# Chunked attention in 256-token units with one head per half of the array's rows, ahead of a soft mixture of experts

## The chip, the cores and the metric

The kernel runs on one core of a Trainium2 chip. The core has five engines with their own instruction queues: TensorE (in profiles PE for matmuls and PEld for weight loads), VectorE (DVE), ScalarE (ACT), GpSimd (POOL) and SyncE (SP), which here only issues DMA transfers. Sixteen DMA engines move data between HBM and SBUF. Matmuls write PSUM, eight banks of 2 KB on each of 128 partitions. The metric is the device time of one execution in microseconds; less is better.

## What is computed

All data is fp32: 4 batches, 8 heads, 768 tokens, head dimension 64. The first half is attention in chunks of 32 queries. A chunk sees 8 memory keys of its head and the tokens from 16 before the chunk to 8 after it, 64 keys in all away from the sequence's ends.

```python
for c in range(nc):                                  # 24 chunks of 32
    l_start = max(0, c_start - left_ctx)             # 16 before
    r_end = min(S, c_end + right_ctx)                # 8 after
    k_full = np.concatenate([mem_k, k[:, :, l_start:r_end]], axis=2)
    v_full = np.concatenate([mem_v, v[:, :, l_start:r_end]], axis=2)
    scores = scale * np.matmul(q_c, k_full.transpose(0, 1, 3, 2))
    a = softmax(scores)
    out[:, :, c_start:c_end] = np.matmul(a, v_full)
```

The second half takes the 3072 tokens x (512 wide) through 8 experts with 4 slots each:

```python
logits = x @ phi                                     # 3072 x 32
d = softmax over tokens (axis 0); slot_input = d.T @ x
h = np.maximum(slot_input[e] @ w1[e], 0.0)           # 512 -> 1024, per expert
slot_out[e] = h @ w2[e]                              # 1024 -> 512
return softmax over slots (axis 1) of logits @ slot_out
```

The two weight arrays have 16.8 MB each, the output 6.3 MB.

## The kernel before

The attention loop (line 362) runs over 24 units of 128 tokens, four chunks each, with all eight heads. Keys lie in `k_slab` with the two heads of a pair interleaved over the 128 partitions (`par`), and each head's columns hold zeros on the other head's partitions. So one matmul in `scores` (line 218) contracts over 128 rows and gives the scores of two heads for one chunk: 32 queries by 2 x 64 keys, into a strip of 32 output partitions. There are 16 such matmuls per unit, four head pairs by four chunks. `values` (line 271) is built in the same way with `v_slab`. Per unit follow: four transposes of the probabilities (`transpose_p`, copied out of PSUM by ScalarE), the row maximum, the subtraction, the sum and its reciprocal on VectorE, the exponent on ScalarE, the normalization into `x_slab` on VectorE and four transposes of x. Every fourth unit there are logits and, one and two units later, the dispatch of four units' tokens with a running maximum per slot.

Neighbouring chunks share value rows. `share_v` (line 129) copies 64 partitions of a unit, on VectorE for even units and on ScalarE for odd ones.

PE, DVE, ACT and SP keep the order in which the program is written (`InOrder`); GpSimd's few operations and all waits come from the framework, which puts semaphores on data. `scores(i + 2)` runs two units ahead of `values(i)`.

All loads are issued by SP in one order. Inputs arrive as queries for two units (`load_q`), keys for three (`load_k`, two transfers on every other partition each) and values for two (`load_v`, four transfers on every other partition). At the end of each iteration `load_w` issues weight pieces of 512 KB: 13 slabs are free from the start, filled at 0.9 piece per unit, and from unit 18 on the input slabs that are no longer needed are taken as well, 38 pieces in all. The other 26 wait until the experts have read the pieces of w1 whose slabs they take.

At the start GpSimd, VectorE and ScalarE clear the padded slabs (lines 188 to 198). After the loop come the last group's dispatch (lines 400 to 453), the experts' first layer (`expert_in`), the combine weights, and per half of the output columns the second layer (`expert_out`) and the combine, which ends in the output transfers. `keep_warm` puts matmuls on zeros between them.

```python
load_w(usable[i] if i >= NU - 6 else min(NW, W0 + int(WRATE * max(0, i + 1 - WSTART))))
```

Of the kernel before, what the change touches and what calls it, by code (L numbers as in the profile page):

```python
# [10 lines left out]
F32 = mybir.dt.float32  # L11
# [10 lines left out]
CPU = P // CHUNK  # L22
UPB = S // P
NU = B * UPB
HALF_U = 3
NHALF = NU // HALF_U
SPAN_STEP = CPU // 2 * (NMEM + 2 * CHUNK)
SPAN_EXTRA = LEFT + RIGHT
STREAM = (S // CHUNK // 2) * (NMEM + 2 * CHUNK) + SPAN_EXTRA
HALF_W = HALF_U * SPAN_STEP + SPAN_EXTRA  # L30
# [12 lines left out]
PIECE = 1024  # L43
NW = 13
NV = 3
W0 = 1
SHARE_MOD = 2
SHARE_DVE = 1
WARM0 = 3
FILL = (4, 2, 6, 2, 2)  # L50
WARM1 = 1
# [19 lines left out]
def window_start(c):  # L71
    return (c // 2) * (NMEM + 2 * CHUNK) + (c % 2) * CHUNK


@with_exitstack
def tile_attn_softmoe(
    ctx: ExitStack,
    tc: tile.TileContext,
    qT: bass.AP,
    kT: bass.AP,  # L80
    vw: bass.AP,
# [7 lines left out]
    pe, dve, act, sp = (InOrder(tc, e) for e in (nc.tensor, nc.vector, nc.scalar, nc.sync))  # L89
    cp = ctx.enter_context(tc.tile_pool(name="cp", bufs=1))  # L90
    wk = ctx.enter_context(tc.tile_pool(name="wk", bufs=2))
    ps = ctx.enter_context(tc.tile_pool(name="ps", bufs=2, space=bass.MemoryType.PSUM))

    k_slab = [cp.tile([P, 2, NPAIR, HALF_W], F32, tag=f"k{i}", name=f"k{i}") for i in range(2)]
    v_slab = [cp.tile([P, 2, 2, 2, 2, NPAIR, D], F32, tag=f"v{i}", name=f"v{i}") for i in range(NV)]
    q_slab = [cp.tile([P, 2, NPAIR, P], F32, tag=f"q{i}", name=f"q{i}") for i in range(3)]
# [4 lines left out]
    hT = cp.tile([P, E, NFC, NSLOT], F32, tag="hT", name="hT")  # L101
# [4 lines left out]
    phi_sb = cp.tile([P, NKC, NSLOT], F32, tag="phi", name="phi_sb")  # L106

    def load_q(p):
        sp.dma_start(q_slab[p % 3], qT[p])

    def load_k(hb, lo=0, hi=HALF_W):
        b, half = divmod(hb, 2)
        off = half * HALF_U * SPAN_STEP - LEFT
        if half and lo == 0:
            nc.gpsimd.tensor_copy(
                out=k_slab[1][:, :, :, 0:SPAN_EXTRA], in_=k_slab[0][:, :, :, HALF_W - SPAN_EXTRA:HALF_W]
            )
        lo = max(lo, SPAN_EXTRA if half else LEFT)
        hi = min(hi, HALF_W - RIGHT if half else HALF_W)
        for par in range(2):  # L120
            sp.dma_start(k_slab[half][par:P:2, par, :, lo:hi], kT[b, :, par, :, off + lo:off + hi])
# [495 lines left out]
```

## Time and profile before

| | us |
|---|---|
| median of 3 runs | 190.63 |
| lowest and highest | 189.44, 194.12 |
| profiled execution, first to last instruction | 193.7 |
| PE busy in it | 154.5 |
| DVE busy | 122.1 |
| ACT busy | 77.9 |
| POOL busy | 19.4 |

The profile lists one execution by its span; the time of that execution as a whole is not listed apart from the three runs. TensorE's mean granted clock was 0.942 of full speed. 63.11 MB went through the DMA queues at a mean of 326 GB/s.

The page cuts the span into 40 slices and gives each engine's busy share in tenths. A group line names the engine, the operation, what it writes and reads (out<-in), the shapes and the count, then busy time, mean ns of one, and the idle time ahead of it with what ended that. "issue" as a releaser means that the engine waited for nothing that the profile shows. Matmul ends are modelled, so times between the starts of neighbouring groups are the safer measure. Nearly all operations carry line 66, that of the helper which records them; they are told apart by tile names: s scores, p probabilities, pt their transposes, a values, x and xT tokens, l logits, D dispatch, h and so the experts' two layers, o the combine.

### The profile page before, as it was taken

The page shows a single profiled execution, that of the slowest core. Times are in us where ns is not written, and L with a number is a line of the kernel's source. Part 1 is how long each engine was busy: PE and PEld are TensorE (multiplying, and loading weights), DVE is VectorE, ACT ScalarE, POOL GpSimd, SP SyncE. Part 2 cuts the span into 40 slices and gives each one's busy share as a digit, 9 for nine tenths or more (in the row PEclk, how much of TensorE's full clock was granted, in tenths as well). Part 3 has the DMA queues.
Part 4 walks back from the last instruction along what each step waited for, and adds up shares of the span by engine and source line. Part 5 has one row for each costly group of instructions (what it writes and reads, how often), then busy time and mean ns, then how long its engine had stood idle before and what let it go on. Part 6 is the DMA issues. An engine that isn't in the chain of part 4 may idle for free.

```text
span 193.7 us, 6125 instructions
## 1 busy us (share of the span) xinstructions
PE 154.5 (80%) x2637; PEld 108.0 (56%) x2637; DVE 122.1 (63%) x249; ACT 77.9 (40%) x137; POOL 19.4 (10%) x22
## 2 busy tenths in 40 slices
PE   6733997859996969989579996999899769599540
PEld 3313775737684737757457684767466535365330
DVE  4699999829999649989936997243742220370550
ACT  8003457415756434763445577220322220160240
POOL 8991000000000000000000000000311100000000
PEclk9995899978999999999978999999999978999995
DMA  5999969998899999889978999999999999999296
GB/s 154 305 276 285 287 188 292 343 320 298 278 279 329 344 337 326 254 271 354 261 231 240 335 394 418 409 405 409 412 405 409 409 407 408 409 415 401 85 376 273
DMA packets 21194, 63.11 MB, mean 326 GB/s; under 512 B 2992, under 2 KB 7600, under 8 KB 21168
## 3 DMA queue, kind: packets, MB, share of 16 engines
q1 hardware_dynamic: 21168, 62.73, 92.8%
q8 instruction: 21, 0.34, 0.8%
q14 instruction: 5, 0.04, 0.1%
HBM read 56.43 MB, written 6.29 MB: 324 GB/s over the span
## 4 chain that ended last, share of the span: by engine, by line
PE 45%; DMA 23%; DVE 15%; issue 7%; POOL 3%; ACT 2%; SPq 1%; POOLq 0%
PE s L66 8%; PE a L66 8%; DMA k<-in_kT_dram 6%; DMA w<-in_w_dram 5%; PE xt_ps L66 5%; DMA v<-in_w_dram 5%; DVE z L66 4%; PE h L66 4%; PE so L66 4%; PE pt_ps L66 4%; DMA v<-in_vx_dram 3%; PE o L66 3%; PE D_ps L66 3%; DMA v<-in_vw_dram 3%; DVE v L66 3%
## 5 line engine op out<-in xcount | busy, mean ns | idle before, releaser
L66 PE MATMUL s<-k,q 128*32 128x128 f32 x768 | 28.8, 291 | 6.6 <-issue 4.2
L66 PE MATMUL a<-v,pt 128*32 128x128 f32 x768 | 27.8, 281 | 1.9 <-ACT pt L66 1.1
L66 PEld LDWEIGHTS s<-k,q 128*32 128x32 f32 x768 | 22.1, 117 | 12.1 <-issue 9.9
L66 PEld LDWEIGHTS a<-v,pt 128*32 128x32 f32 x768 | 21.4, 113 | 8.3 <-issue 6.4
L66 ACT COPY xT<-xt_ps 128x512 f32<-128x512 f32 x24 | 14.0, 584 | 29.2 <-PE xt_ps L66 28.9
L66 ACT ACTIVATE p<-p 128x512 f32<-128x512 f32 x24 | 15.1, 629 | 25.1 <-DVE p L66 25.1
L66 PE MATMUL pt_ps<-ident,p 128*128 128x128 f32 x96 | 16.7, 299 | 6.2 <-ACT p L66 6.2
L66 PE MATMUL xt_ps<-ident,x 128*128 128x128 f32 x96 | 16.4, 293 | 6.0 <-issue 4.4
L66 DVE TENSOR_TENSOR x<-a,z 128x512 f32<-128x512 f32 x24 | 16.5, 688 | 5.6 <-PE a L66 5.1
L66 DVE TENSOR_REDUCE mx<-s 128x8 f32<-128x512 f32 x24 | 16.1, 670 | 5.2 <-PE s L66 4.9
L66 PEld LDWEIGHTS pt_ps<-ident,p 128*128 128x128 f32 x96 | 10.7, 147 | 11.7 <-issue 11.7
L66 DVE TENSOR_TENSOR p<-s,mx 128x512 f32<-128x512 f32 x24 | 16.6, 693 | 0.8
L66 ACT COPY pt<-pt_ps 128x512 f32<-128x512 f32 x24 | 13.9, 578 | 8.0 <-PE pt_ps L66 8.0
L66 DVE TENSOR_REDUCE z<-p 128x8 f32<-128x512 f32 x24 | 16.3, 681 | 0.8
L66 PEld LDWEIGHTS xt_ps<-ident,x 128*128 128x128 f32 x96 | 10.4, 143 | 11.1 <-issue 7.5
L66 ACT COPY v<-v 64x1024 f32<-64x1024 f32 x12 | 12.5, 1046 | 0.3
L193 POOL MEMSET v<- 128x4096 f32 x3 | 10.5, 3513 | 0.0
L66 PE MATMUL o<-shl,cst 128*128 128x256 f32 x48 | 7.6, 302 | 3.0 <-DVE shl L66 2.9
L66 DVE COPY so_sb<-so 128x256 f32<-128x256 f32 x2 | 0.8, 425 | 14.1 <-PE so L66 14.1
L473 POOL COPY c<-c_sb 128x512 f32<-128x512 f32 x6 | 3.6, 614 | 60.3 <-DVE c_sb L66 48.0
L66 PEld LDWEIGHTS o<-shl,cst 128*128 128x128 f32 x48 | 6.3, 189 | 4.8 <-ACT shl L66 3.6
L66 PE MATMUL D_ps<-x,dT 128*32 128x512 f32 x48 | 7.4, 604 | 1.8 <-issue 1.6
(101 smaller groups left out, 195.1 us busy)
## 6 DMA issues: line engine op xcount, KB each, us to landing
w<-in_w_dram SPq DMA_DIRECT2D x26, 512.0 KB, 9.1
v<-in_w_dram SPq DMA_DIRECT2D x16, 512.0 KB, 10.2
q<-in_qT_dram SPq DMA_DIRECT2D x12, 512.0 KB, 7.2
v<-in_vw_dram SPq DMA_DIRECT2D x24, 256.0 KB, 6.6
k<-in_w_dram SPq DMA_DIRECT2D x12, 512.0 KB, 9.5
out_dram<-v SPq DMA_DIRECT2D x8, 512.0 KB, 5.2
k<-in_kT_dram SPq DMA_DIRECT2D x8, 424.0 KB, 8.5
v<-in_vx_dram SPq DMA_DIRECT2D x24, 128.0 KB, 6.7
```

The source lines that it names most:

```text
L66: return self.tc.keep_in_program_order(f(*args, **kwargs))
L193: nc.gpsimd.memset(v_slab[i], 0.0)
L473: nc.gpsimd.tensor_copy(out=c4, in_=c_sb[:, 4 * G:4 * G + 4, :].rearrange("p u (o s) -> p u o s", o=1).broadcast_to([P, 4, 4, NSLOT]),)
```

## The change

The loop runs over 12 units of 256 tokens. Keys, queries and values of a unit lie in one row per partition of `in_slab`, head 0 of each pair on partitions 0 to 63 and head 1 on 64 to 127, without zeros. A matmul of `scores` and `values` now contracts over the 64 rows of one head and gives 64 columns; there are 64 of each per unit. Scores and values of the two heads go to different PSUM banks. `scores` reverses the halves of the key window for some chunks, to match the order in which the value rows lie.

A unit is loaded by one transfer over all partitions (two for the first unit) and a second one of the extra value rows on partitions 32 to 95. Shared value rows are copied by GpSimd, two copies of 32 partitions per unit. Three slabs are in flight; unit n+3 is loaded at the end of iteration n. The reductions and the reciprocal work on 256 tokens at a time; subtractions, exponents and normalizations stay at 128. `scores(n + 1)` runs one unit ahead of `values(n)`. The clearing of the slabs is gone; hT is cleared later, on GpSimd. gsum's copy goes from VectorE to GpSimd.

Weight pieces have 1 MB, in 12 slabs and 8 more that come free late. The loop issues 1, 1, 2, 2, 3, 3, 3 and 4 of them in total by the end of iterations 0 to 7, then 13, 15, 17 and 18. One filler burst after the loop shrinks from 4 to 2. The rest of the dispatch, the experts and the combine issue the same operations, with other buffers.

Below are the new lines; the removed ones stand in the listing above.

```diff
+UU = 2
+NUNIT = NU // UU
+UNITS_B = UPB // UU
+PAIRS = UU * CPU // 2
+KW = PAIRS * STEP + LEFT + RIGHT
+KQ = NPAIR * KW
+QW = UU * NPAIR * P
+VW = UU * 2 * NPAIR * D
+ROW = KQ + QW + VW
...
-PIECE = 1024
-NW = 13
...
-W0 = 1
...
-WRATE = 0.9
-WSTART = 2
+PIECE = 2048
+NW = 12
+NIN = 3
...
+    in_slab = [cp.tile([P, ROW + VW], F32, tag=f"in{i}", name=f"in{i}") for i in range(NIN)]
...
+    warm = cp.tile([P, 512], F32, tag="warm", name="warm")
+
+    k_in = [t[:, 0:KQ].rearrange("p (g n) -> p g n", g=NPAIR) for t in in_slab]
+    q_in = [t[:, KQ:KQ + QW].rearrange("p (u g n) -> p u g n", u=UU, g=NPAIR) for t in in_slab]
+    v_in = [
+        t[:, KQ + QW:].rearrange("p (o u c g d) -> p o u c g d", o=2, u=UU, c=2, g=NPAIR) for t in in_slab
+    ]
+
+    def load_in(n):
+        t = in_slab[n % NIN]
+        if n == 0:
+            sp.dma_start(t[:, 0:KQ + QW], kqv[n, :, 0:KQ + QW])
+            sp.dma_start(t[:, KQ + QW:ROW], kqv[n, :, KQ + QW:ROW])
         else:
...
+            sp.dma_start(t[:, 0:ROW], kqv[n])
+        sp.dma_start(t[32:96, ROW:ROW + VW], vx[n])
+
+    def share_v(n):
+        v = v_in[n % NIN]
+        for r in (0, 96):
+            pool.tensor_copy(out=v[r:r + 32, 1], in_=v[r:r + 32, 0])
...
+    freed = [(n - 1, in_slab[n % NIN][:, 0:PIECE]) for n in range(NUNIT - NIN, NUNIT)]
+    freed += [(n, in_slab[n % NIN][:, PIECE:2 * PIECE]) for n in range(NUNIT - NIN, NUNIT)]
+    freed += [(NUNIT + i, x_slab[i].rearrange("p u n -> p (u n)")) for i in range(2)]
+    for since, ap in sorted(freed, key=lambda f: f[0]):
+        slabs.append(ap)
+        for i in range(since, NUNIT + 2):
             usable[i] = len(slabs)
 
-    pieces = [("w1", e, kc) for e in range(E) for kc in range(NKC)]
-    pieces += [("w2", blk, e, h) for blk in range(NBLK) for e in range(E) for h in range(2)]
+    pieces = [("w1", e, h) for e in range(E) for h in range(2)]
+    pieces += [("w2", blk, e) for blk in range(NBLK) for e in range(E)]
+    n_w1 = 2 * E
...
     make_identity(nc, ident)
...
+    w_ps = ps.tile([P, 512], F32, tag="L", name="warm_ps")
+    for _ in range(3):
+        pe.matmul(w_ps, lhsT=warm[:, 0:P], rhs=warm, start=True, stop=True)
+
+    load_in(0)
     sp.dma_start(phi_sb, phi.rearrange("(kc p) s -> p kc s", p=P))
...
+    load_in(1)
+    load_in(2)
+    load_w(1)
...
+    def scores(n):
+        k, q = k_in[n % NIN], q_in[n % NIN]
+        s_ps = ps.tile([P, 2, UU, NPAIR, NKEY], F32, tag="S", name=f"s{n}")
+        for uu in range(UU):
+            for g in range(NPAIR):
+                for h in range(2):
+                    hs = slice(D * h, D * h + D)
+                    for j in range(CPU):
+                        w0 = (2 * uu + j // 2) * STEP + CHUNK * (j % 2)
+                        win = k[hs, g, w0:w0 + NKEY]
+                        if (h == 0) != (j % 2 == 1):
+                            win = win.rearrange("p (t n) -> p t n", t=2)[:, ::-1, :]
+                        pe.matmul(
+                            s_ps[32 * j:32 * j + 32, h, uu, g, :],
+                            lhsT=q[hs, uu, g, 32 * j:32 * j + 32], rhs=win,
+                            start=True, stop=True,
+                        )
         return s_ps
 
...
+    def softmax(n, s_ps):
+        if n % UNITS_B == 0:
+            for h, c in ((0, CHUNK), (1, 0)):
+                dve.memset(s_ps[0:32, h, 0, :, c:c + LEFT], NEG)
+        if n % UNITS_B == UNITS_B - 1:
+            for h, c in ((0, CHUNK), (1, 0)):
+                dve.memset(s_ps[96:128, h, UU - 1, :, c + CHUNK - RIGHT:c + CHUNK], NEG)
+        mx = wk.tile([P, 2, UU, NPAIR], F32, tag="mx", name=f"mx{n}")
+        dve.tensor_reduce(
+            out=mx.rearrange("p h u g -> p (h u g)"), in_=s_ps.rearrange("p h u g n -> p (h u g) n"),
+            axis=AX.X, op=ALU.max,
         )
...
+        p = wk.tile([P, UU, NPAIR, 2, NKEY], F32, tag="p", name=f"p{n}")
+        for uu in range(UU):
+            dve.tensor_tensor(
+                out=p[:, uu].rearrange("p g h n -> p h g n"), in0=s_ps[:, :, uu],
+                in1=mx[:, :, uu].rearrange("p h (g o) -> p h g o", o=1).broadcast_to([P, 2, NPAIR, NKEY]),
+                op=ALU.subtract,
+            )
+        pexp[n] = p
...
+    def values(n, pts):
+        v = v_in[n % NIN]
+        a_ps = ps.tile([P, 2, UU, NPAIR, D], F32, tag="A", name=f"a{n}")
+        for uu in range(UU):
+            for g in range(NPAIR):
+                for h in range(2):
+                    hs = slice(D * h, D * h + D)
+                    for j in range(CPU):
+                        pe.matmul(
+                            a_ps[32 * j:32 * j + 32, h, uu, g, :],
+                            lhsT=pts[uu][hs, g, 32 * j:32 * j + 32],
+                            rhs=v[hs, j % 2, uu, j // 2, g, :],
+                            start=True, stop=True,
+                        )
         return a_ps
 
...
+    def normalize(n, a_ps):
+        x = x_slab[n // 2 % 2][:, n % 2 * UU:n % 2 * UU + UU, :]
+        for uu in range(UU):
+            dve.tensor_tensor(
+                out=x[:, uu].rearrange("p (g h d) -> p h g d", h=2, d=D),
+                in0=a_ps[:, :, uu],
+                in1=rz[n][:, uu].rearrange("p g (h o) -> p h g o", o=1).broadcast_to([P, 2, NPAIR, D]),
+                op=ALU.mult,
+            )
...
+    softmax(0, scores(0))
+    exponent(0)
     share_v(0)
...
     a_ps = None
...
+    for n in range(NUNIT):
+        Gl = (n - 3) // 2 if n >= 3 and n % 2 == 1 else None
+        Gd = (n - 4) // 2 if n >= 4 and n % 2 == 0 else None
+        pts = transpose_p(n)
+        if n >= 1:
+            normalize(n - 1, a_ps)
+        if n + 1 < NUNIT:
+            share_v(n + 1)
+        if Gl is not None:
+            l_ps = logits(Gl)
+        if n + 1 < NUNIT:
+            s_ps = scores(n + 1)
+        normalizer(n)
+        if n >= 1:
+            transpose_x(2 * n - 2)
+        if n + 1 < NUNIT:
+            softmax(n + 1, s_ps)
+        if Gl is not None:
+            dispatch_max(Gl, l_ps)
+        a_ps = values(n, pts)
+        if n >= 1:
+            transpose_x(2 * n - 1)
+        if n + 1 < NUNIT:
+            exponent(n + 1)
+        if Gl is not None:
+            dispatch_exp(Gl, l_ps)
+            dispatch_t(Gl)
+        if Gd is not None:
+            D_ps = dispatch(Gd)
+            dispatch_z(Gd)
+            dispatch_sum(Gd, D_ps)
+        if n + NIN < NUNIT:
+            load_in(n + NIN)
+        load_w(usable[n] if n >= NUNIT - 4 else 1 + 2 * (n + 1) // 5)
+    normalize(NUNIT - 1, a_ps)
...
+    hT = [wk.tile([P, E // 2, NFC, NSLOT], F32, tag="p", name=f"hT{i}") for i in range(2)]
+    for i in range(2):
+        pool.memset(hT[i], 0.0)
```

More of the change, by code (lines that the diff above doesn't have):

```diff
@@ L165, in load_w @@
             if kind == "w1":
-                sp.dma_start(s, w1[at[0]].rearrange("(p kc) f -> p kc f", kc=NKC)[:, at[1], :])
-            else:
-                sp.dma_start(s, w2[at[0], at[1], :, at[2]])
-    def span(t):
-        lo = 0 if t == 0 else t * SPAN_STEP + SPAN_EXTRA
-        return lo, (t + 1) * SPAN_STEP + SPAN_EXTRA
-    warm = cp.tile([P, 512], F32, tag="warm", name="warm")
-    def warm_up(n):
-        w_ps = ps.tile([P, 512], F32, tag="L", name="warm_ps", bufs=1)
-        for _ in range(n):
-            pe.matmul(w_ps, lhsT=warm[:, 0:P], rhs=warm, start=True, stop=True)
@@ new lines, in transpose_p @@
+    def transpose_p(n):
+        pts = []
+        for uu in range(UU):
+            t_ps = ps.tile([P, NPAIR, P], F32, tag="T", name=f"pt_ps{n}_{uu}", bufs=2)
+            for g in range(NPAIR):
+                pe.transpose(t_ps[:, g, :], pexp[n][:, uu, g].rearrange("p h n -> p (h n)"), ident)
+            pt = wk.tile([P, NPAIR, P], F32, tag="pt", name=f"pt{n}_{uu}", bufs=3)
+            act.copy(out=pt, in_=t_ps)
+            pts.append(pt)
+        return pts
+    def values(n, pts):
+        v = v_in[n % NIN]
+        a_ps = ps.tile([P, 2, UU, NPAIR, D], F32, tag="A", name=f"a{n}")
+        for uu in range(UU):
+            for g in range(NPAIR):
+                for h in range(2):
[7 more added lines that the diff above has]
+                        )
+        return a_ps
@@ L290, in transpose_x @@
+    def normalize(n, a_ps):
+        x = x_slab[n // 2 % 2][:, n % 2 * UU:n % 2 * UU + UU, :]
+        for uu in range(UU):
+            dve.tensor_tensor(
[3 more added lines that the diff above has]
+                op=ALU.mult,
+            )
     def transpose_x(u):
[L291 removed]
+        t_ps = ps.tile([P, NKC, P], F32, tag="X", name=f"xt_ps{u}")
@@ L402, in tile_attn_softmoe @@
+    normalize(NUNIT - 1, a_ps)
+    D_ps = dispatch(NG - 2)
+    dispatch_z(NG - 2)
+    dispatch_sum(NG - 2, D_ps)
+    load_w(usable[NUNIT])
+    keep_warm(2)
+    transpose_x(NU - 2)
     transpose_x(NU - 1)
-    keep_warm(FILL[1])
+    keep_warm(2)
     l_ps = logits(NG - 1)
@@ L527, in tile_attn_softmoe @@
         combine_weights(G)
+    n_slab = len(slabs)
+    late = len(pieces) - n_slab
+    spare = [i for i in range(n_w1) if i >= late] + list(range(n_w1, n_slab)) + list(range(late))
+    stage = [slabs[i].rearrange("p (o u n) -> p o u n", o=2, n=WB)[:, o] for i in spare for o in range(2)]
     def expert_out(blk):
@@ L550, in expert_out @@
         return shl
-    n_slab, n_w1 = len(slabs), E * NKC
-    held = {i % n_slab for i in range(n_w1, len(pieces))}
-    order = [i for i in range(n_slab) if i not in held] + [i % n_slab for i in range(n_w1, n_w1 + 2 * E)]
-    stage = [slabs[i].rearrange("p (u n) -> p u n", n=WB) for i in order]
     def combine(blk, shl):
```

315 lines of the change are left out of this document (74 added, 241 removed).

## The prediction

> **What bounds the kernel now.** I read the page's header, the chain that ended last, the groups kept apart by shape, the timeline of TensorE, then busy time and DMA queues by stretch.
>
> ```profile
> span 193.7 us, 6125 instructions
> PE 154.5 (80%) x2637; PEld 108.0 (56%) x2637; DVE 122.1 (63%) x249; ACT 77.9 (40%) x137; POOL 19.4 (10%) x22
> PE   6733997859996969989579996999899769599540
> DVE  4699999829999649989936997243742220370550
> GB/s 154 305 276 285 287 188 292 343 320 298 278 279 329 344 337 326 254 271 354 261 231 240 335 394 418 409 405 409 412 405 409 409 407 408 409 415 401 85 376 273
> q8 instruction: 21, 0.34, 0.8%
> 51.05 1.00 PE D_ps L66 x8
> 123.14 1.09 PE fill_ps L66 x8
> 139.07 3.59 PE h L66 x64
> 172.46 7.09 PE so L66 x128
> 179.57 0.43 DVE so_sb L66
> 17.55 1.08 PE L66 MATMUL pt_ps<-ident,p 128*128 128x128 f32 x4 [6.17 <-ACT p L66]
> ```
>
> The span has four parts. The start lasts until the first transpose of probabilities at 17.55. The attention loop runs to 123.14, where the filler matmuls begin: 105.6 us, or 8.8 for two units of 128 tokens. Dispatch takes 15.9, to the first expert matmul at 139.07, and the experts and the combine 54.6, to 193.7. In the loop TensorE and VectorE are both near nine tenths and DMA moves about 300 GB/s; afterwards it moves 408 while TensorE works through h, so and o.
>
> Queue 8 carries the instructions. TensorE has 2637 matmuls and 2637 weight loads, so 21 transfers make one for about 250 of them.
>
> ```profile
> 41.38 1.51 PE L66 MATMUL s<-k,q 128*32 128x128 f32 x24 [2.37 <-issue]
> 59.10 0.85 PE L66 MATMUL a<-v,pt 128*32 128x128 f32 x21
> 60.77 0.63 PE L66 MATMUL a<-v,pt 128*32 128x128 f32 x11 [0.82 <-issue]
> 66.51 1.08 PE L66 MATMUL s<-k,q 128*32 128x128 f32 x32
> 67.52 0.66 PE L66 MATMUL xt_ps<-ident,x 128*128 128x128 f32 x4
> 68.10 1.05 PE L66 MATMUL D_ps<-x,dT 128*32 128x512 f32 x2
> 70.72 0.63 PE L66 MATMUL D_ps<-x,dT 128*32 128x512 f32 x3 [1.57 <-issue]
> 41.38:59.95 18.57, 18.57 (x380) 0.91 0.92 292
> 60.77:69.15 8.38, 7.16 (x126) 1.00 1.04 340
> 70.72:82.37 11.65, 11.65 (x254) 1.00 0.95 306
> ```
>
> In the last three rows (stretch, length, busy time with matmuls, clock, DMA share, GB/s) each stretch ends at a stop put down to issue, in the middle of a burst with nothing to wait for. They hold 380, 126 and 254 matmuls and as many weight loads: 760, 252 and 508 instructions, which with a few semaphore instructions are 3, 1 and 2 times 256. So TensorE stops at block borders of 256 instructions, waiting for code. The queue, asked by stretch:
>
> ```profile
> q8 instruction: 1, 0.02, 5.9%
> q8 instruction: 1, 0.02, 5.8%
> 126.80:139.67 12.87, 11.57 (x128) 1.00 1.03 408
> 139.67:147.70 8.03, 8.03 (x133) 1.00 1.02 407
> 160.64:172.87 12.23, 10.16 (x134) 0.99 1.02 408
> ```
>
> The first row is the answer for 38.6 to 40.0 and for 128.9 to 130, the second that for 45.1 to 46.3, 67.9 to 69.4 and 142 to 143.1; between 40.0 and 45.1, 61 and 67.8, 139.7 and 142 no such row comes. A share of 5.9% of 16 engines over 1.4 us is one engine for 1.3 us. So the code of a block is fetched only after the border before it has been passed: after 41.38 at 45.1, after 60.77 at 67.9. It lands by 40.0 and 69.3, and TensorE goes on at 41.38 and 70.72, 1.4 later. I call the time from a border to the next block being usable F. It was 9.95 from 60.77 to 70.72 and 46.3 + 1.4 - 41.4 = 6.3 after 41.4. Late, where all loads cross all partitions, borders lie at 126.80, 139.67 and 160.64: F = 130.0 + 1.4 - 126.8 = 4.6 and 143.1 + 1.4 - 139.7 = 4.8; the fetch after 160.64 (161.1 to 162.3) gives 3.0.
>
> **The change, part by part.** Instructions first. 16 score matmuls of a unit leave 32 rows each of matmuls and weight loads (s x768 in 24 units), so a matmul is four instructions. Per 256-token unit the new kernel has 64 matmuls for the scores and 64 for the values, 512 instructions; 16 transposes add 32, logits and dispatch (every second iteration) 41: 585, with semaphores some 595, or 2.32 blocks. The old one spends 329, or 1.3 blocks, on the same tokens. One iteration therefore takes at least 2.32 F.
>
> Rate of the engines, from these groups:
>
> ```profile
> L66 PE MATMUL s<-k,q 128*32 128x128 f32 x768 | 28.8, 291 | 6.6 <-issue 4.2 <-DMA k<-in_kT_dram 2.4
> L66 DVE TENSOR_REDUCE mx<-s 128x8 f32<-128x512 f32 x24 | 16.1, 670 | 5.2 <-PE s L66 4.9
> L66 DVE TENSOR_TENSOR p<-s,mx 128x512 f32<-128x512 f32 x24 | 16.6, 693 | 0.8
> L66 ACT ACTIVATE p<-p 128x512 f32<-128x512 f32 x24 | 15.1, 629 | 25.1 <-DVE p L66 25.1
> L66 DVE COPY v<-v 64x1024 f32<-64x1024 f32 x12 | 8.3, 690 | 0.4
> L66 DVE TENSOR_REDUCE stats<-l 128x1 f32<-128x128 f32 x6 | 1.5, 248 | 2.5 <-PE l L66 2.5
> L66 DVE RECIPROCAL z<-z 128x8 f32<-128x8 f32 x24 | 4.9, 203 | 0.8
> L66 DVE TENSOR_SCALAR z<-z 128x8 f32<-128x8 f32 x24 | 4.2, 176 | 0.8
> L473 POOL COPY c<-c_sb 128x512 f32<-128x512 f32 x6 | 3.6, 614 | 60.3 <-DVE c_sb L66 48.0
> L194 POOL MEMSET hT<- 128x2048 f32 x1 | 1.8, 1804 | 0.0
> L66 DVE COPY gsum<-sel 128x128 f32<-128x128 f32 x1 | 8.3, 8291 | 0.0
> ```
>
> - TensorE. 32 instructions of 128 columns take 1.01 us (66.51 to 67.52), 31.5 ns each in four column strips; 64 instructions of 256 columns took 3.59, 56 ns: time goes with columns. With 64 columns, and heads in two row halves, an instruction costs 31.5/2 = 15.8 ns if the halves take turns, 7.9 if they run side by side, 31.5 if columns no longer matter. Scores and values of an iteration are 256 matmul instructions: 4.0, 2.0 or 8.1 us (now 4.0). Transposes take 0.58 for four (67.52 to 68.10), 2.3 for 16; logits (32 like the scores) and dispatch (1.00 for eight) come every second time and add 1.1. I take 15.8: 7.4 us. A gain beyond that would hide behind F.
> - VectorE loses 12 copies (8.3 us), 24 pairs of small operations, halved (12 x 0.38 = 4.5), and the fixed cost of 24 merged reductions: from 248 ns at 128 elements and 670 at 512, 1024 take 1233, 0.11 less than two, 2.6 in all. That is 15.4 of the loop's 105.6, so 7.5 per iteration if VectorE set every pair; nothing else is added to it. ScalarE loses its 12 copies and stays under both.
> - GpSimd gains two copies of 1024 elements on 32 partitions per unit: at 614 ns for 512, 2.5 us at most per iteration, issued one iteration ahead; they land behind the previous unit's values. If that cover failed the cost would be 2.5 per iteration.
> - The loop's own chain: transposes 1.2, half of logits 0.25, scores 2.0, maximum 1.23, two subtractions 1.39, last exponent 0.63, six hand-overs of 0.1: 7.3. The score tile has a single buffer, but softmax has read it an iteration before.
> - Input DMA. 1.95 MB per unit pair as before, but one transfer across all partitions. At 408 GB/s, with 0.4 weight pieces of 1 MB, 5.8 us per iteration. SP waits for the values of unit n before it loads unit n+3, with the weights queued behind; 1.5 iterations remain for the landing. Not binding above 5.8.
> - Start. The memsets of padded slabs go. gsum's copy, 8.29 us while GpSimd cleared the slabs, held VectorE from the first maximum; the scores had begun at 6.87. With 1.2 MB to land first I keep 6.9, then 1.6 scores at the early clock, 1.2 maximum, 0.7 and 0.6: transposes at 11.0, 6.5 earlier.
> - After the loop the same operations in the same order; piece size and slabs change, 21 MB of 33.5 fit before the experts free any. hT is now cleared on GpSimd ahead of its copies of c, 1.8 us in a wait for c_sb that lasted 48.0. I leave 15.9 and 54.6, within 2 either way, since h, so and o keep their instructions.
>
> F is the open price: 3.0 at best, 9.95 at worst, both with DMA busy. In the new loop all loads but one are full-partition, like those of the late stage, and DMA would be busy for 5.8 of 10 us. I take 4.3, just under the late 4.6 and 4.8. Then 2.32 x 4.3 = 10.0 per iteration, above 7.3, 7.4 and 7.5. (After the stop of 2.37 us the stretch shows a mean clock of 0.91, after the shorter ones 1.00; if each stop halved the clock for a while that would come on top, and belongs to the upper end.) Sum: 11.0 + 120 + 15.9 + 54.6 = 201.5 of span. The 193.7 of before stands 3.1 above the median of 190.63, so I forecast 198.
>
> [...]
>
> **The rivals.**
> 1. [...] Chance 0.20.
> 2. F near its floor, 3.1 to 3.9, because large transfers leave gaps: 7.5 to 9.0 per iteration, 168 to 187. For it: the 3.0 after 160.64, in the fullest DMA stage. Chance 0.22.
> 3. The row halves do not do what the change says: 64 columns cost what 128 did. 8.1 + 3.4 = 11.5 per iteration, 81.5 + 138 = 219.5, or 216. It decides from 9.35 per iteration, 23 ns an instruction. Against it: time went with columns from 256 to 128. Chance 0.16. [...] No run here shows columns this few.
>
> Forecast, F of 4.0 to 5.2: 190 to 223, chance 0.42.
>
> **The numbers.** Break-even is 9.35 per iteration, F = 4.03. A measurement of this kernel tells about 2% from no change, 186.8 to 194.4, F of 3.89 to 4.17. Forecast: slower 0.38, same 0.04. Rival 1: faster 0.20. Rival 2: faster 0.18, same 0.04. Rival 3: slower 0.10, same 0.05, faster 0.01. Together faster 0.39, same 0.13, slower 0.48. The range runs from 167, just under rival 1, to 222, F = 5.16; outside lie the worst of the forecast and what rival 1 may gain in the start or the tail.
>
> **What would show it.** In the changed profile, right: some 33 transfers on queue 8; stops put down to issue inside s and a, a border every 4.3 us; 10 us per iteration; first transposes near 11. Wrong: 7.5 per iteration with VectorE without gaps (rival 1); score bursts of 64 instructions at 2 us without stops inside (rival 3); or a tail other than 70.5 us from the loop's end.

## The result, and the profile after

The changed kernel takes 232.09 us (median of 4 runs, 230.27 to 235.88), the kernel before 191.62 (4 runs, 189.44 to 194.12). The ratio is 1.215, with a 95% interval of 1.198 to 1.232: slower, and by more than the forecast of 198 and its range (to 222) allowed. Medians are of all runs; ratios and their intervals leave out executions more than 1.5% slower than the fastest of the same kernel. The profiled execution of the changed kernel took 230.93 with a span of 229.2, so 1.7 us lie outside the span.

From the page of the changed kernel: header, engines, four rows of the timeline, the instruction queue, and the groups of scores and values.

```profile
span 229.2 us, 8977 instructions
PE 161.9 (71%) x4167; PEld 114.7 (50%) x4167; DVE 98.0 (43%) x194; ACT 62.0 (27%) x124; POOL 31.4 (14%) x39
PE   7474557755787488468694646969979959579672
DVE  1454636542269347274384440632472131440251
PEclk9977967587589559755796577799999999958955
GB/s 240 420 423 176 306 128 221 226 303 173 174 77 419 103 280 180 166 61 412 108 402 423 425 426 418 429 363 174 183 326 425 428 420 425 184 367 187 0 275 274
q8 instruction: 32, 0.52, 0.9%
L62 PE MATMUL a<-in,pt 64*32 64x64 f32 x1536 | 24.2, 261 | 24.6 <-issue 24.6
L62 PE MATMUL s<-in 64*32 64x64 f32 x1536 | 21.8, 270 | 4.3 <-issue 3.3
```

Before, TensorE and VectorE were busy nine tenths of the loop and DMA moved about 300 GB/s. Now all three have gaps: VectorE's work fell from 122.1 to 98.0 us and it often waits, and DMA drops as low as 61 GB/s in the loop. What fills the gaps stands behind the group of the values: 24.6 us of waiting for "issue". Queue 8 brought 32 transfers in place of 21.

The parts of the span, from TensorE's timeline of the changed kernel (start, length, group, and in brackets the idle time ahead of it with what ended it):

```profile
6.62 1.49 PE L62 MATMUL s<-in 64*32 64x64 f32 x128
11.27 1.16 PE L62 MATMUL pt_ps<-ident,p 128*128 128x128 f32 x8 [3.17 <-ACT p L62]
...
72.02 0.74 PE L62 MATMUL a<-in,pt 64*32 64x64 f32 x50
76.32 1.38 PE L62 MATMUL a<-in,pt 64*32 64x64 f32 x78 [3.56 <-issue]
...
136.63 1.96 PE L62 MATMUL a<-in,pt 64*32 64x64 f32 x119 [3.12 <-issue]
138.52 1.07 PE L62 MATMUL xt_ps<-ident,x 128*128 128x128 f32 x4
139.53 1.05 PE L62 MATMUL D_ps<-x,dT 128*32 128x512 f32 x5
142.82 1.92 PE L62 MATMUL D_ps<-x,dT 128*32 128x512 f32 x3 [2.25 <-issue]
...
153.01 0.71 PE L62 MATMUL fill_ps<-warm 128*128 128x128 f32 x4
...
164.67 3.66 PE L62 MATMUL h<-w,siT 128*32 128x256 f32 x64
```

The same borders in the kernel before:

```profile
123.06 1.16 PE L66 MATMUL fill_ps<-warm 128*128 128x128 f32 x8
...
133.87 3.66 PE L66 MATMUL h<-w,siT 128*32 128x256 f32 x64
```

The second of these corrects the prediction: 139.07 was the second burst of h, the first begins at 133.87. Dispatch took 10.8 before and the tail 59.8; their sum, 70.6, is what it was.

| us | before | after | change | forecast |
|---|---|---|---|---|
| start, to the first transposes | 17.55 | 11.27 | -6.3 | 11.0 |
| loop, to the first filler | 105.5 | 141.7 | +36.2 | 120 |
| dispatch, to the first h | 10.8 | 11.7 | +0.9 | 10.8 |
| tail | 59.8 | 64.5 | +4.7 | 59.8 |

The four changes make 35.5, the difference of the spans. By the forecast's span of 201.5 the miss is 27.7: 0.3 in the start, 21.7 in the loop, 5.7 behind it.

The stops are the ones foretold. From 136.63 to 142.82 TensorE ran 119 + 4 + 5 = 128 matmuls and as many weight loads, 256 instructions, one block. Between 140 and 141.5 one transfer was on queue 8, and about 1.4 us after its end the engine went on. Counted every 256 instructions, 26 blocks run from 7.5 to 149.0, 5.44 us each; F, from a border to the next usable block, was 3.2 to 6.4, on average 4.74. At 16 of the 26 TensorE stood until the code came, and these blocks took 4.86 on average. The other 10 took longer for their own work and waits, 6.39. That is 16 x 4.86 + 10 x 6.39 = 141.7, as long as the loop (the 26 blocks begin and end some 4 us before it).

Busy time of the engines in the loop, TensorE's granted clock, DMA share and GB/s, for the changed kernel, then for the kernel before:

```profile
11.30:153.00 141.70, 95.72 (x3333) 72.51 (x3333) 69.54 (x129) 42.58 (x88) 24.69 (x24) 0.74 0.70 272
```

```profile
17.50:123.00 105.50, 90.58 (x1865) 67.68 (x1865) 84.48 (x182) 56.14 (x101) 1.04 (x3) 0.95 0.94 305
```

The clock fell from 0.95 to 0.74. Three neighbouring blocks of the changed kernel in the same columns: one of its own length, one that ends in a stop of 3.56, and the one after that stop:

```profile
65.70:70.50 4.80, 4.59 (x121) 2.96 (x124) 2.87 (x5) 2.74 (x5) 0.00 (x0) 1.00 0.73 245
70.50:76.30 5.80, 2.26 (x149) 1.84 (x143) 4.11 (x11) 0.58 (x1) 2.07 (x2) 0.85 0.77 320
76.30:83.40 7.10, 5.01 (x126) 4.10 (x126) 2.94 (x5) 3.33 (x9) 0.00 (x0) 0.50 0.64 235
```

After the stop the whole next block runs at half clock. It needs 5.01 us of work and stands 2.07 more for the exponents of the dispatch (the wait ahead of `dt_ps`), so its 7.1 us are its own. Four of the ten blocks, this one among them, look like this, and six of the ten show a clock of 0.50 to 0.53.

### The profile page after: what moved, and what is told of

Same layout as the page of the kernel before. It is cut to its first block, busy times and chain, and to the rows that moved or that the text cites. A ratio compares the mean times of both kernels' runs of the same rounds, so it can differ in the third digit from the quotient of the medians.

```text
span 229.2 us, 8977 instructions
## 1 busy us (share of the span) xinstructions
PE 161.9 (71%) x4167; PEld 114.7 (50%) x4167; DVE 98.0 (43%) x194; ACT 62.0 (27%) x124; POOL 31.4 (14%) x39
## 4 chain that ended last, share of the span: by engine, by line
PE 63%; issue 16%; ACT 11%; DMA 5%; DVE 3%; SPq 1%; ACTq 0%; DVEq 0%
PE a L62 10%; PE s L62 9%; PE xt_ps L62 8%; PE pt_ps L62 8%; PE so L62 6%; PE h L62 5%; DMA in<-in_kqv_dram 5%; PE oS L62 4%; PE l L62 3%; PE D_ps L62 3%; ACT in L62 3%; ACT p L62 3%; ACT xT L62 3%; PE fill_ps L62 1%; PE ct_ps L62 1%
## 5 line engine op out<-in xcount | busy, mean ns | idle before, releaser
L62 PE MATMUL a<-in,pt 64*32 64x64 f32 x1536 | 24.2, 261 | 24.6 <-issue 24.6
L62 POOL COPY in<-in 32x1024 f32<-32x1024 f32 x24 | 24.8, 1034 | 94.8 <-DMA in<-in_kqv_dram 84.7
L62 PEld LDWEIGHTS a<-in,pt 64*32 64x32 f32 x1536 | 19.6, 123 | 28.8 <-issue 28.6
L62 PE MATMUL s<-in 64*32 64x64 f32 x1536 | 21.8, 270 | 4.3 <-issue 3.3
L62 PEld LDWEIGHTS s<-in 64*32 64x32 f32 x1536 | 19.2, 126 | 8.9 <-issue 7.6
L62 DVE TENSOR_REDUCE z<-p 128x16 f32<-128x1024 f32 x12 | 14.6, 1215 | 9.0 <-ACT p L62 9.0
L62 DVE TENSOR_REDUCE mx<-s 128x16 f32<-128x1024 f32 x12 | 14.7, 1225 | 8.3 <-PE s L62 8.0
L62 ACT COPY pt<-pt_ps 128x512 f32<-128x512 f32 x24 | 13.8, 586 | 15.9 <-PE pt_ps L62 15.8
L62 DVE TENSOR_TENSOR p<-s,mx 128x512 f32<-128x512 f32 x24 | 15.5, 686 | 0.4
L62 PE MATMUL h<-w,siT 128*32 128x256 f32 x192 | 11.0, 381 | 0.8 <-ACT hs L62 0.8
L62 PE MATMUL so<-w,hT 128*32 128x256 f32 x192 | 11.4, 397 | 0.0
L62 DVE COPY in<-o 128x512 f32<-128x512 f32 x12 | 8.1, 690 | 7.4 <-PE o L62 7.4
```

Of the source, the lines that this page charges most:

```text
L62: return self.tc.keep_in_program_order(f(*args, **kwargs))
```

## Experiments

**Fewer instructions, same columns.** First the cause itself. The diff is shown for the scores; the values are edited alike, and `half_scores` has the edit of the scores alone. Both kernels compute pairs 1 and 3 with the operand of pairs 0 and 2, so they serve for their time only.

```diff
-            for g in range(NPAIR):
+            for g in range(0, NPAIR, 2):
...
-                        win = k[hs, g, w0:w0 + NKEY]
+                        win = k[hs, g:g + 2, w0:w0 + NKEY]
...
-                            s_ps[32 * j:32 * j + 32, h, uu, g, :],
+                            s_ps[32 * j:32 * j + 32, h, uu, g:g + 2, :],
```

> The changed kernel, but each matmul of scores and values now covers two head pairs: the queries (or probabilities) of pair g meet the 128 columns of keys (or values) of pairs g and g+1. So pairs 1 and 3 are computed with the operand of pairs 0 and 2; columns, transposes, transfers and everything else stay, and only the instructions fall, from about 595 to 335 per iteration, 1.3 blocks in place of 2.32. Theory (waiting for code sets the loop, 11.8 us for 2.32 blocks = 5.1 per block): 1.3 x 5.1 = 6.6, so VectorE and the chain (7.3 to 7.5, at worst the 8.8 of the kernel before) take over: the loop falls from 141.7 to 90-106 us and the total from 232 to 181-197. Rival (matmuls on 64 rows, or the chain of one 256-token unit with a single score buffer, are slow in themselves): the columns are the same, so the loop stays near 140 and the total at 225-235.

> The changed kernel with only the matmuls of the scores covering two head pairs (pairs 1 and 3 are scored with the queries of pairs 0 and 2); the values keep 64 matmuls per unit. Instructions per iteration fall from about 595 to 465, 1.82 blocks. Theory (each block costs the loop about 5.1 us, in proportion): 1.82 x 5.1 = 9.3 per iteration, a loop of 108-114 us, a total of 199-206. Rival (a threshold: once the code of an iteration is a little shorter it arrives in time, as with 1.3 blocks): a loop near the 98.8 of 1.3 blocks, total 188-194.

With both halved the total was 189.03 us (187.2 to 190.86; the kernel before, run beside it, 193.88), with the scores alone 213.29, ratio 1.102 (1.087 to 1.116). The loops, first with both halved, then with the scores alone:

```profile
11.00:109.80 98.80, 75.40 (x1862) 55.08 (x1862) 69.36 (x129) 42.61 (x88) 24.71 (x24) 0.83 0.86 339
```

```profile
11.00:131.40 120.40, 84.32 (x2629) 62.91 (x2629) 70.73 (x129) 42.62 (x88) 24.70 (x24) 0.81 0.77 300
```

1862, 2629 and 3333 matmuls take 98.8, 120.4 and 141.7 us; with both halved the loop is within the 90 to 106 of the theory of code. The rival of the first run, slow row halves or a slow 256-token chain, is out: the same columns over the same rows in the same units run 43 us faster. Between the two theories of the second run the middle point decides for neither: 10.0 per iteration is more than the 9.3 of a cost in proportion and more than the 8.2 of a threshold. Per iteration 8.2, 10.0 and 11.8 lie on a line, 3.5 us per block more, that does not go through zero. That fits two kinds of blocks: in the middle run, 10 of 20 blocks stopped for code (5.1 us each) and 10 took 6.2 for their own work.

**More instructions in the kernel before.** The converse, with none of the change's other parts (the scores are shown, the values are edited alike):

```diff
-                pe.matmul(
-                    s_ps[32 * j:32 * j + 32, 2 * g:2 * g + 2, :],
...
-                    rhs=k[:, :, g, w0:w0 + NKEY],
+                for h in range(2):
+                    pe.matmul(
+                        s_ps[32 * j:32 * j + 32, 2 * g + h, :],
...
+                        rhs=k[:, h, g, w0:w0 + NKEY],
```

> The kernel before with each matmul of scores and values of 128 columns cut into two of 64 columns, one per head: the same operands, columns, results and transfers, twice the instructions for scores and values (about 335 to 595 per two units). Theory (code): the loop goes from 105.6 to 12 x 2.32 x 5.1 = 140 us, the total from 191 to 226 (215-235), with stops put down to issue inside s and a. Rival (the new kernel is slow for its row halves, its unit or its transfers): nothing of that is here, 188-197.

229.05 us, ratio 1.196 (1.154 to 1.239). Its loop and two of its groups:

```profile
15.80:154.40 138.60, 103.17 (x3337) 82.73 (x3337) 86.05 (x182) 57.02 (x101) 1.57 (x3) 0.91 0.74 239
```

```profile
L66 PE MATMUL s<-k,q 128*32 128x64 f32 x1536 | 32.9, 232 | 20.0 <-issue 19.5
L66 PE MATMUL a<-v,pt 128*32 128x64 f32 x1536 | 33.5, 236 | 11.9 <-issue 11.9
```

The split alone makes the loop 33.1 us longer, and 31.4 us of waiting for issue stand ahead of s and a, where the kernel before had 4.2 ahead of s and 0.8 ahead of a. So the number of instructions is enough to turn the old kernel's loop into the new one's (138.6 against 141.7). The clock was 0.91 here and 0.74 in the changed kernel, for nearly the same loop.

**The clock, and the row halves.** Matmuls on all 128 rows, in scores and values; everything else as in the changed kernel:

```diff
-                    hs = slice(D * h, D * h + D)
+                    hs = slice(0, P)
```

> The changed kernel with each matmul of scores and values contracting over all 128 rows in place of the 64 of its head (so each result is the sum over both heads of a pair). Instructions, columns, transfers and waits are the same; the two row halves no longer run side by side. In the changed kernel six of the ten blocks that don't wait for code run at a clock of 0.50 to 0.53 and need 5 us of work; in the kernel before with split matmuls, of 128 rows, the clock was 0.91 with as many stops. Theory A (the lower clock goes with matmuls on 64 rows, and costs the loop in the blocks that don't wait for code, by an estimate from their rows some 14 us): clock 0.88-0.95 in the loop, those blocks at 4.6-5.5 in place of 6.4, loop 126-134, total 216-225. Theory B (the clock falls after every stop, whatever the rows): clock near 0.74, loop 140-148. Theory C (the clock rises and the time stays: what is gained goes into longer stops and into the matmuls, which no longer share the array): clock about 0.9, loop 138-144.

234.52 us, ratio 1.206 (1.188 to 1.224); loop 141.3, from the first transposes at 12.07. The loop, with a little on either side:

```profile
11.50:155.00 143.50, 102.68 (x3341) 84.69 (x3341) 71.35 (x131) 43.30 (x90) 24.72 (x24) 0.87 0.68 267
```

Theory C, with a clock of 0.87, a little below its 0.9. The clock goes with the rows: 0.87 against 0.74 with the same program but for the rows. In this loop the clock fell to 0.50 for 3.4 us at a time; in the changed kernel's, for 3.4 to 13.7 (from 95.1 to 108.8 without a break). And the time doesn't go with the clock. Blocks of their own length fell from 6.39 to 5.8, those that stop rose from 4.86 to 5.15, TensorE was busy for 7 us more (102.7 against 95.7) and stood 26.4 us for issue in place of 32.4. The estimate of 14 us was therefore not confirmed: this run takes the cheaper row halves (the first 128 matmuls of the scores took 1.49 us in the changed kernel and 1.99 here) away together with the lower clock, so it bounds what the two do together, which is nothing. It says as much of the change: using the two row halves, its new way through the array, was worth nothing in a loop that waits for code.

**A wait inside a loop that waits for code.**

```diff
             dispatch_exp(Gl, l_ps)
-            dispatch_t(Gl)
+            if n == NUNIT - 1:
+                dispatch_t(Gl)
...
+        if Gd is not None:
+            dispatch_t(Gd)
         normalizer(n)
```

> The changed kernel with the transpose of the dispatch exponents issued one iteration later, behind that iteration's first transposes of x; in the trace of the changed kernel TensorE waits for ScalarE ahead of it five times, 9.3 us in all. Theory (a loop that waits for code: the wait lies within the time in which the next block is fetched): the waits vanish from the rows, stops put down to issue grow by most of it, and the loop stays within 3 of 141.7, the total within 4 of 232. Rival (waits add to the code): loop 132-135, total 222-225.

231.76 us, ratio 1.196 (1.182 to 1.210); loop 140.0. TensorE's groups with their idle time in the loop, the changed kernel, then this one:

```profile
L62 PE MATMUL pt_ps<-ident,p 128*128 128x128 f32 x96 | 20.1, 377 | 6.0 <-ACT p L62 6.0
L62 PE MATMUL dt_ps<-ident,d 128*128 128x128 f32 x5 | 2.2, 447 | 9.3 <-ACT d L62 9.3
```

```profile
L62 PE MATMUL a<-in,pt 64*32 64x64 f32 x1536 | 23.0, 249 | 28.2 <-issue 28.2
L62 PE MATMUL pt_ps<-ident,p 128*128 128x128 f32 x96 | 19.7, 370 | 10.8 <-ACT p L62 10.8
L62 PE MATMUL dt_ps<-ident,d 128*128 128x128 f32 x5 | 2.2, 444 | 1.0 <-ACT d L62 1.0
```

Of the wait of 9.3 us 8.3 are gone, and the loop is only 1.7 shorter. As much came back elsewhere: 3.6 as waiting for code ahead of a (24.6 to 28.2) and 4.8 ahead of the next transposes, which wait for ScalarE's exponents. Waits do not add to the code; but that more than half of the wait moved to another place in the chain, and not to the code, had not been in the expectation.

**What sets F.** Two kernels take transfers away from the loop:

```diff
-        load_w(usable[n] if n >= NUNIT - 4 else 1 + 2 * (n + 1) // 5)
+        load_w(1)
```

> The changed kernel with no weight piece issued inside the loop after the first (17 of 18 wait until the loop is over; the tail has to wait for them and grows by some 30-45 us, so the loop's time is what counts). DMA then carries 1.95 MB of inputs per iteration alone. Theory A (F, the time from a border to the next usable block, is long because the fetch stands behind the loop's other transfers): F falls from 4.7 to 3.5-4.0 and the loop from 141.7 to 100-115. Theory B (F is the queue's own latency): F stays at 4.5-5 and the loop at 135-143.

and the same with

```diff
-        if n + NIN < NUNIT:
-            load_in(n + NIN)
```

> The changed kernel without any load inside the loop: only the first three units are brought in, units 3 to 11 compute on their data again, and the weights after the first piece wait for the end of the loop. Instructions of TensorE are the same. Theory (F is a latency of 3.4 to 4.1 us when DMA is idle at the border, and what lies above that is waiting behind the kernel's own transfers): every F of the loop after its first 30 us lies at 3.4-4.2, stops are shorter, and the loop falls from 141.7 to 112-122. Rival (the time lies elsewhere, in the halved clock and in waits): 130-140.

Without weights in it the loop took 134.0 us (226.32 in all) and F was 4.5 on average: at or a little below the bands of theory B, far from A's, since the input transfers alone keep DMA busy at many borders. Border by border the rows split cleanly: where DMA was idle, the fetch began 1.0 to 1.6 us after the border; where it was busy throughout, 2 to 4 us after.

Without any loads the loop took 121.4, inside the theory's band (213.82 in all, one run). Not as expected, DMA was not idle all along: with no load to wait for, SP issued the weights of the tail at once, and DMA was busy until 44 us and again from about 104. That makes the comparison within one run. Its stretches from border to border:

```profile
20.70:38.60 17.90, 11.40 (x382) 9.28 (x384) 8.46 (x15) 4.54 (x8) 4.14 (x4) 0.60 1.01 423
53.60:100.40 46.80, 34.17 (x1402) 26.70 (x1403) 30.20 (x57) 18.93 (x41) 10.35 (x10) 0.88 0.02 4
```

The first holds three blocks (382 matmuls and 384 weight loads) at DMA's full rate, 5.97 us each; the second eleven blocks with DMA idle, 4.25 each, F at 2.7 to 4.1. TensorE runs the same loop in both. So up to some 1.7 us per block are the kernel's own transfers standing in the way of its code (the second stretch also has the logits and dispatch that the first has not).

In the changed loop every fetch began only 0.8 to 4.0 us after a border, so while a block of 256 instructions ran, just the next one was being brought. At 4.25 to 5.97 us per block, a block of 128 matmuls of 64 columns hides less than half of its successor's fetch: 128 matmuls of the scores take 1.49 us in the changed kernel at a clock of 1.00 and 2.06 at 0.50.

**Whether the size of the packets matters.** Loads in pieces of at most 4 KB per partition:

```diff
-        if n == 0:
...
-        else:
-            sp.dma_start(t[:, 0:ROW], kqv[n])
+        for c in range(0, ROW, ROW // 4):
+            sp.dma_start(t[:, c:c + ROW // 4], kqv[n, :, c:c + ROW // 4])
...
-                sp.dma_start(s, w2[at[0], at[1]])
+                for k in range(2):
+                    sp.dma_start(s[:, F * k:F * k + F], w2[at[0], at[1], :, F * k:F * k + F])
```

> The changed kernel with the same bytes loaded in packets of at most 4 KB: each unit's transfer is cut into four of 824 columns (3.3 KB per partition), each weight piece into two of 1024 (4 KB). In the changed kernel the packets have 13.2 and 8.2 KB and take 0.49 and 0.31 us; in the kernel before those of the weights have 4 KB and take 0.16. With all DMA engines busy the fetch of a block began 3.3 to 4.0 us after the border in the changed kernel, 1.8 to 2.4 late in the kernel before; with DMA idle, 1.0 to 1.7. Theory A (the fetch stands behind a number of packets on its engine, so that its delay goes with their size): the delay with busy DMA falls to 2-2.5, F at a stop from 4.9 to 4.0-4.3, the loop from 141.7 to 122-134, the total to 212-224. Theory B (the size plays no part): loop 137-143, total 226-235.

233.66 us, ratio 1.215 (1.204 to 1.225), loop 142.5, F on average 4.7 and delays mostly of 3.3 to 3.9 with DMA busy throughout. Theory A falls: between these two sizes, that of the packets plays no part.

**Why the late stage showed a shorter F.** The prediction took F from the rows of h, where DMA is as full.

```diff
-            for kc in range(NKC):
+            for c, kc in [(c, kc) for c in range(0, 256, 64) for kc in range(NKC)]:
...
-                        t[32 * j:32 * j + 32, e2, :],
+                        t[32 * j:32 * j + 32, e2, c:c + 64],
...
-                        rhs=wt[:, 256 * j:256 * j + 256],
+                        rhs=wt[:, 256 * j + c:256 * j + c + 64],
```

> The changed kernel with each matmul of the experts' first layer (256 columns, 56 ns) cut into four of 64 columns with the same weights loaded again: the same products and the same transfers in a stage where the weights keep all DMA engines busy, but short instructions and about nine blocks of code more. In the late stage of both kernels the fetch began 1.8 to 3.2 us after a border, in the loop of the changed kernel with DMA as busy 3.3 to 4.0. Theory A (the engine asks for code ahead of what it executes, so slow instructions make F look shorter, and the rows of the late stage were the wrong ones to take F from): with short instructions the delay in this stage rises to 3.2-4.0 and F at its stops to 5.5-6.4. Theory B (the late stage's fetches are quicker in themselves): delay 1.8-2.6, F 4.2-5. Either way the total rises, by about nine blocks, to 255-280.

257.27 us in one run. TensorE's timeline in the first layer:

```profile
172.18 1.53 PE L62 MATMUL h<-w,siT 128*32 128x64 f32 x93 [0.21 <-ACT hs L62]
177.39 3.64 PE L62 MATMUL h<-w,siT 128*32 128x64 f32 x128 [3.68 <-issue]
...
195.27 1.30 PE L62 MATMUL h<-in,siT 128*32 128x64 f32 x75
200.73 3.20 PE L62 MATMUL h<-in,siT 128*32 128x64 f32 x128 [4.15 <-issue]
```

The stage now stops in the middle of its bursts, as the loop does. Seven borders stopped, with F of 5.5 on average; of their fetches five began 3.1 to 4.9 us after the border, one with DMA idle after 0.8, and one with DMA busy after 1.5, which neither theory has. Theory A fits better, though three delays are above its band: measured from the execution of a border, F looks shorter where the instructions are slow. That the engine asks for code ahead of what it executes is inferred from this; no row shows the asking itself.

**The combine.** In the changed kernel, the end of the first half of the combine, with the r before it:

```profile
196.38 0.70 PE L62 MATMUL r<-so_sb,gsum 128*128 128x256 f32 x2 [0.55 <-DVE so_sb L62]
...
204.04 0.80 PE L62 MATMUL oS<-shl,cst 128*128 128x256 f32 x2 [0.25 <-ACT in L62]
204.64 0.63 PE L62 MATMUL o<-shl,cst 128*128 128x256 f32 x2
205.56 0.80 PE L62 MATMUL oS<-shl,cst 128*128 128x256 f32 x2 [0.29 <-ACT in L62]
206.28 7.78 PE L62 MATMUL so<-w,hT 128*32 128x256 f32 x128
```

In the kernel before, the same stretch:

```profile
166.43 0.70 PE L66 MATMUL r<-so_sb,gsum 128*128 128x256 f32 x2 [0.55 <-DVE so_sb L66]
168.58 3.88 PE L66 MATMUL o<-shl,cst 128*128 128x256 f32 x24 [1.45 <-DVE shl L66]
172.39 1.50 PE L66 MATMUL so<-w,hT 128*32 128x256 f32 x24
```

From r to the next so it took 6.0 before and 9.9 after. From the second on, every pair of matmuls into oS waits 0.25 to 0.44 us for ScalarE's copy of the pair before it; two of them share one PSUM tile of two banks, and the next pair takes the same place. Two remedies:

```diff
-                pair = ps.tile([P, 2, 2, WB], F32, tag="S", name=f"oS{blk}_{G}")
+                pair = ps.tile([P, 2, 2, WB], F32, tag="SA"[G // 2 % 2], name=f"oS{blk}_{G}")
```

> The changed kernel with the combine's paired PSUM tile taken in turn from two places (tag S and tag A, each of two banks) in place of S alone. Theory (the 4 us that each half of the combine takes longer than in the kernel before come from TensorE and ScalarE taking turns on the one pair tile): each half falls from 10.4 to about 6.6 us, the total by 7 (6-8.5) to 225. Rival (half the clock, or ScalarE's or SP's own rate, holds the combine): the total stays within 2 of 232.

and a tile for each copy:

```diff
-            if G % 2 == 0:
-                pair = ps.tile([P, 2, 2, WB], F32, tag="S", name=f"oS{blk}_{G}")
+            one = ps.tile([P, 2, WB], F32, tag="SA"[G % 2], name=f"oS{blk}_{G}")
...
-                    c_ps = pair[:, G % 2]
+                    c_ps = one
```

> The changed kernel with a PSUM tile of its own for each copy by ScalarE in the combine, in turn from tag S and tag A, in place of the pair tile. Theory (TensorE and ScalarE take turns on the pair tile; in the first half of the combine that is on the path, in the second the output transfers set the end): from r to the next so 9.9 falls to 6-6.5 us, no wait for ScalarE ahead of oS in it, from the second r to the end stays at 13.5-15; the total falls by 3-4. Rival (half the clock holds the combine): from r to so stays above 8.

The first did not do what was expected of it: 231.64 us (226.31 to 234.29), from r to so 8.2, since two copies still share a tile. With a tile each:

```profile
192.39 0.70 PE L62 MATMUL r<-so_sb,gsum 128*128 128x256 f32 x2 [0.55 <-DVE so_sb L62]
...
198.02 0.40 PE L62 MATMUL oS<-shl,cst 128*128 128x256 f32 x2
199.09 7.11 PE L62 MATMUL so<-w,hT 128*32 128x256 f32 x128 [0.68 <-ACT in L62]
```

6.7 from r to so, no wait for ScalarE ahead of oS in it, and 13.45 from the second r to the end (14.6 in the changed kernel). So 3.2 of the 3.9 us go with the shared tile. Its two runs lie far apart, 221.96 and 230.14, too wide for a gain of 4 to be read from the totals. Together with the small packets:

> The kernel with packets of at most 4 KB and, in the combine, a PSUM tile of its own for each of ScalarE's copies, in turn from tag S and tag A. Theory: the gain of the combine, 4 us, adds to that of the packets: 4 below the run with small packets alone; still slower than the kernel before, since 2.3 blocks of code per iteration remain. Rival (the tail gives it back to the output transfers): no gain beside that run.

230.64 us, ratio 1.188 (1.175 to 1.201). That is 3.0 less than the small packets alone by the medians and, by the ratios (1.188 against 1.215), 5 less. The two intervals do not overlap (up to 1.201, from 1.204), so a gain is there, of the size of the expected 4 as far as these runs tell; and the kernel is still far slower than the one before. In its profile r to so took 7.6, and the last of its pairs of matmuls into o and oS took 0.63 us each in place of 0.40. In the changed kernel they do the same in this stretch, where the clock was 0.73 on average against 1.00 in the kernel before, so the clock has a share in it too.

**The start alone.** The part of the change that the prediction credited with 6.5 us, done in the kernel before:

```diff
-    dve.tensor_copy(out=gsum, in_=sel.rearrange("p (o s) -> p o s", o=1).broadcast_to([P, 4, NSLOT]))
+    nc.gpsimd.tensor_copy(out=gsum, in_=sel.rearrange("p (o s) -> p o s", o=1).broadcast_to([P, 4, NSLOT]))
```

> The kernel before with one copy moved: gsum goes from VectorE to GpSimd, behind its memsets. Theory (the prediction's term of the start: gsum's copy of 8.29 us held VectorE from the first maximum): the first transposes come at 11-13.5 in place of 17.55 and the total falls by 4-6.5 to 185-187. Rival (the first keys, or the code of the second block, would hold the start anyway): transposes stay after 16 and the total at 189-192.

```profile
10.69 0.63 PE L66 MATMUL pt_ps<-ident,p 128*128 128x128 f32 x4
37.07 1.10 PE L66 MATMUL pt_ps<-ident,p 128*128 128x128 f32 x4
12.01 7.63 DMA v<-in_vx_dram
25.74 6.31 DMA k<-in_kT_dram
```

The first transposes come 6.9 us earlier, a little more than the theory said, and the total does not follow: 193.17 us over 10 runs against 193.88 over 14, and a ratio of 1.013 (1.001 to 1.026): no gain in either. Mechanism right, gain lost. The trace of the profiled execution, the fastest of the ten, shows where: the transposes of the first six units begin at 10.69, 16.56, 23.07, 26.82, 30.06 and 37.07, in the kernel before at 17.55, 21.56, 25.49, 28.69, 32.37 and 37.12. By the sixth unit the lead is gone. The chain that ended last runs there (the last two rows) over the landing of value rows until 19.64 and of keys until 32.05, with a stop for issue up to 33.34: an earlier start only waits for its loads.

None of these kernels that compute the whole result beats the one before. The one with half the instructions is level with it or a little faster, but leaves out part of the computation.

## Why the prediction was wrong in size and right in direction

- **Start, 11.0.** Right: 11.27, with the scores at 6.62 and 1.49 us long.
- **Blocks: 33 transfers, 2.32 per iteration.** Nearly right: 32, and 26 blocks in the loop, 2.17 per iteration. Stops inside s and a, put down to issue: right. That code is fetched one block ahead, on which the forecast stood: held, every fetch of the loop on queue 8 began 0.8 to 4.0 us after a border. That the number of instructions sets the loop is shown from both sides, by halving and by splitting the matmuls.
- **F = 4.3, "just under the late 4.6 and 4.8".** This term was too small: 4.74 on average, 4.86 where it was waited for. The argument for it, that full-partition transfers would make the loop like the late stage, failed: at the borders of the loop with DMA busy throughout, F was 5.7 on average. The run with short instructions in the late stage gave 5.5 there. 26 x (4.74 - 4.3) is 11 of the 21.7 us.
- **10.0 per iteration as the larger of code, chain and engines.** This step failed: the loop took 11.8 per iteration. The maximum holds block by block, not iteration by iteration: ten blocks were too long for it, by waits for exponents and by their work at half clock, and the time that the fetch had over in them could not be saved for the next block, since only one is fetched ahead. They took 10 x (6.39 - 4.55) = 18 us beyond their own F, which was 4.55. With 26 blocks where 27.8 were counted (1.8 x 4.3 = 8 less), 11 + 18 - 8 makes the 21.7. The halved clock after stops, which the prediction left to the upper end, is part of these 18: six of the ten had 4.7 to 6.1 us of work at 0.50 to 0.53. How large a part stays open, since the only run with a higher clock also lost the row halves.
- **Engines.** TensorE's 7.4 per iteration became 8.0 busy (95.72 / 12) at a clock of 0.74; VectorE's 7.5 was an upper bound, 5.8 busy (69.54 / 12); GpSimd's copies stayed hidden (24.69 us in the loop, none on the chain). None set the loop.
- **Dispatch and tail, 70.5 within 2.** Wrong by 5.7. "The same operations in the same order" was true, and the buffers had changed: 3.9 lies between the first r and the next so, 3.2 of it by the pair tile of the combine, which the diff showed and the text ahead of the prediction called "other buffers". 0.9 is the dispatch; the rest is spread over the second so, 8.3 us to the next r in place of 7.7 at a clock of 0.92 in place of 1.00, and the second half of the combine, 14.6 in place of 13.7, with 0.9 less up to the first r.
- **Rivals.** The first, code in time and 7.5 us per iteration, and the second, F near 3.1 to 3.9, are out: TensorE stood at 16 of 26 borders, F was 4.74 on average, and even with DMA idle a block cost 4.25. The third, row halves without use, is out too: 128 instructions of 64 columns in 1.49 us are 11.6 ns each, between my two estimates, 7.9 for halves side by side and the 15.8 that I took; on all 128 rows, with all else the same, they took 1.99 us or 15.5 ns each. (The trace of before did hold matmuls of fewer columns than 64, against what the prediction says, but eight of 32 columns, into si_ps, took 1.95 us in all and say nothing of what a burst of 64 columns costs.)
- **From span to time.** 3.1 were taken off because the profiled execution of before lay above its median. In the changed kernel the median lies 2.9 above the profiled span (1.7 outside the span, 1.2 from run to run). These 6 us are the rest of the 34 between 198 and 232.
- **The range.** It ended at F = 5.16 with everything else as forecast: a loop of 12 x 2.32 x 5.16 = 143.7. F stayed inside it, and so did the loop as a whole, 141.7. What carried the time past 222 was the 5.7 behind the loop and the 6 from span to time, for which the range had left no room.

## What to carry to other kernels

Count instructions as a resource: in this loop a block of 256 TensorE instructions cost 4.3 us on average with DMA idle and 6.0 with DMA busy (the run without loads), so a change that cuts columns and doubles matmuls pays only while a block's work is longer than that. Take such a price from a stage with the same kind of instructions and the same DMA load, and add it up block by block. When a description says "other buffers", follow each PSUM tile to the engine that empties it.

## What the runs showed that was not expected

- Code and data share DMA: in the changed loop the fetch of a block began 1.0 to 1.7 us after a border with DMA idle and up to 4 us after with DMA busy, whether the packets had 3 to 4 KB or 8 to 13 KB. In the kernel before it began up to 7.1 us after (border at 60.77, fetch at 67.9) and with its matmuls split up to 5.0; what makes it longest there stays open.
- Matmuls on 64 rows went with a lower granted clock: 0.74 in the changed loop and 0.83 with few stops and half the instructions, against 0.87 for the same loop on 128 rows, 0.91 for the split matmuls and 0.95 before. Why is not shown. After the stop of 3.56 us the next block ran at 0.50.
- A start 6.9 us earlier was worth nothing that could be measured in the kernel before: its lead was gone by the sixth unit.
